# Attention of batches 1 to 3 in steps of two tiles, with q and k turned four tiles at a time

## The chip, the cores and the metric

One core of one Trainium2 chip runs the whole program. The metric is the device time of one execution in microseconds (us); three executions of the kernel before took 1161.79, 1163.22 and 1163.64 us, median 1163.22.

## The reference

The program computes an attention with a sparse mask and feeds its output to a mixture of experts. All data are float32.

```python
# B, H, S, D = 4, 8, 768, 64; n_global, n_local = 8, 96
scores = q @ k.transpose(0, 1, 3, 2) / sqrt(D)
rel = pos[:, None] - pos[None, :]
is_global = pos[None, :] < n_global
is_local = (rel >= 0) & (rel < n_local)
dist = where(is_global & ~is_local, n_local, abs(rel))
scores = where(is_global | is_local, scores - slopes[head] * dist, -1e9)
a = exp(scores - max(scores));  a = a / (sum(a) + 1e-9)
x = (a @ v) -> (B * S, H * D) = (3072, 512)

# E, F = 4, 1024
p = domain_probs / (sum(domain_probs) + 1e-9)
out = sum over e of p[:, e] * (relu(x @ w1[e]) @ w2[e])
```

Since a position looks back at most 95 places and at 8 global columns, a tile of 128 queries needs the 128 keys of its own tile, 96 of the tile before and the global ones: 256 columns.

## The kernel before

**Stages.** The attention of batch 0 runs first (`first_attention`, up to about 60 us). Then the mixture of batches 0 and 1 runs, and the attention of batches 1 to 3 (`attention`, lines 419 to 503) is emitted between its pieces, to about 644 us. The mixture of batches 2 and 3 follows without attention (`turned_batch`). The change touches the middle stage alone.

**The mixture in the middle stage.** A unit is one expert and a quarter of its hidden columns. `first(i)` does seven products of a Strassen-like scheme, each six matmuls of 384 columns into a tile `pm` of the pool `ps_mm` (four buffers, one PSUM bank each); VectorE adds and ScalarE applies the relu. `second(i)` does six groups of six matmuls of 512 columns, each summed by VectorE into `acc`. `first` yields seven times a unit and `second` six times. At these yields the outer loop (lines 1344 to 1377) draws further steps of `attention`: the steps (`count`) are spread evenly over the yields, `span - ONSTEPS` = 385 of them.

**A job of the attention** is one batch and one pair of heads; there are 12. A pair fills the 128 partitions (two heads of 64). q and k are loaded with positions on the partitions and turned by TensorE transposes (`transpose_half`, three tiles at a time, into a buffer of the pool `bank.pt`), then split into a high and a low part in `qs` and `ks` (`prepare_q`, `prepare_k`): ScalarE copies the high part, VectorE subtracts for the low part; once a job VectorE also copies the global keys behind each tile of keys. `scores` does 12 matmuls for two tiles of queries, each from half the array's rows (64 partitions), into two banks of one buffer each (`bank.psa`, `bank.psb`). `softmax` has VectorE add the bias and take the row's extreme, ScalarE take the exponential, VectorE the reciprocal and ScalarE scale. `turn` transposes the weights of one tile (four transposes, two for tile 0) into `bank.pt` (two buffers), and ScalarE copies them to `pT`. `weigh` multiplies three tiles with v, each matmul filling half the array's columns.

**The order in a job.** A step called `flow` handles one tile in each of three states: it emits the scores of a new pair of tiles, then the turn of the tile that is three steps old, then the softmax of the tiles one and two steps old. A job takes 12 steps: q half 0, k half 0, q half 1, tile 0 (with its scores), tile 1, k half 1, an empty step, tile 2 (scores), tile 3, an empty step, tile 4 (scores), tile 5. When six tiles are turned, `leave` emits the 44 products with v; this falls into the next job's step of tile 0, ahead of its scores. The next job's q and k are asked for at the step of tile 5, v at the step of tile 0. All 12 jobs make 149 steps.

**The order on the engines.** The program lists each engine's instructions in one order. In the first stage the code fixes that order itself (`Ordered.on`). From the outer loop's seventh yield on this is off, and the framework's planner orders the instructions by its own cost estimates, with the emitted order as priority.

Of the kernel before, what the change touches and what calls it, by code (L numbers as in the profile page):

```python
# [9 lines left out]
F32 = mybir.dt.float32  # L10
# [4 lines left out]
ALU = mybir.AluOpType  # L15
# [10 lines left out]
def f32(ap):  # L26
    return ap.bitcast(F32)
# [159 lines left out]
def attn_moe_kernel(ctx: ExitStack, tc, q, k, v, n_global, n_local, domain_probs, w1, w2, out):  # L187
# [108 lines left out]
    def load(A, src, b, pr, name):  # L296

        nat = A.nat.tile([P, NQT, 2, D], F32, name=name)
        for j in range(2):
            sy.dma_start(nat[:, :, j, :], src[b, 2 * pr + j].rearrange("(t p) d -> p t d", p=P))  # L300
        return nat

    def transpose_half(A, nat, hf):
        tp = A.pt.tile([P, 512], F32, name="pt")
        for t in range(TPH):
            te.transpose(tp[:, t * P : (t + 1) * P], nat[:, hf * TPH + t].rearrange("p j d -> p (j d)"), ident)
        return tp

    def prepare_q(A, nat, hf, got):

        tp = transpose_half(A, nat, hf)
        if hf == 0:
            got["q"] = A.qs.tile([P, 2, S], F32R, name="qs")
        hi, lo = (got["q"][:, n, hf * HALF : (hf + 1) * HALF] for n in range(2))
        ac.activation(hi, tp[:, :HALF], AF.Copy, scale=-SCALE)
        ve.scalar_tensor_tensor(lo, tp[:, :HALF], -SCALE, f32(hi), op0=ALU.mult, op1=ALU.subtract)

    def prepare_k(A, nat, hf, got):

        tp = transpose_half(A, nat, hf)  # L320
        tpv = tp[:, :HALF].rearrange("p (t c) -> p t c", c=P)
        if hf == 0:
            got["k"] = A.ks.tile([P, 2, NQT, PL], F32R, name="ks")
        ks = got["k"]
        hi, lo = (ks[:, n, hf * TPH : (hf + 1) * TPH, :P] for n in range(2))
        ac.copy(hi, tpv)
        ve.tensor_tensor(lo, tpv, f32(hi), op=ALU.subtract)
        if hf == 0:
            ve.tensor_copy(ks[:, :, :, P:], f32(ks[:, :, 0:1, :NGLOB]).to_broadcast([P, 2, NQT, NGLOB]))

    def scores(ts, got):


        pss = [pool.tile([P, 2, 2 * P], F32, name="ps") for pool in (bank.psa, bank.psb)]
        for i, t in enumerate(ts):
            c0 = max(t - 1, 0) * PL + (0 if t == 0 else NGLOB)
            for n, (qn, kn) in enumerate(((0, 0), (0, 1), (1, 0))):
                for j in range(2):
                    own = slice(j * D, (j + 1) * D)
                    te.matmul(  # L340
                        pss[j][:, i],
                        got["q"][own, qn, t * P : (t + 1) * P],
                        got["k"][own, kn].rearrange("p t c -> p (t c)")[:, c0 : c0 + 2 * P],
                        start=(n == 0),
                        stop=(n == 2),
                    )
        return pss

    def softmax(A, new, old):


        if old:
            pb, zsum = old["pb"], old["zsum"]
        if new:
            t, pr, ps = new["t"], new["pr"], new["ps"]
            cols = slice(0, P) if t == 0 else slice(0, 2 * P)
            bcol = slice(2 * P, 3 * P) if t == 0 else slice(0, 2 * P)
            new["pcol"] = pcol = slice(P, 2 * P) if t == 0 else slice(0, 2 * P)
            nmax = A.small.tile([P, 2], F32, name="nmax")
            new["zsum"] = A.small.tile([P, 2], F32, name="zsum")  # L360
            new["pb"] = A.pb.tile([P, 2, 2 * P], F32, name="pb")
        for j in range(2):
            if new:
                e = new["pb"][:, j, pcol]
                ve.tensor_tensor_reduce(
                    e, ps[j][:, t % 2, cols], bias["n"][:, 2 * pr + j, bcol], 1.0, 3.0e38, ALU.add, ALU.min,
                    nmax[:, j : j + 1],
                )
                ac.activation(
                    e, e, AF.Exp, bias=nmax[:, j : j + 1], scale=-1.0, accum_out=new["zsum"][:, j : j + 1]  # L370
                )
            if old:
                if j == 1:
                    ve.reciprocal(zsum, zsum)
                else:
                    ac.activation(zsum, zsum, AF.Copy, bias=1e-9)
        if old:
            for j in range(2):
                p = pb[:, j, old["pcol"]]
                ac.activation(p, p, AF.Copy, scale=zsum[:, j : j + 1])  # L380

    def turn(bank, A, tile_, copy):

        t, pb = tile_["t"], tile_["pb"]
        pt = bank.pt.tile([P, 2, 2, P], F32, name="pt")
        pT = A.pT.tile([P, 2, 2, P], F32, name="pT")
        w0 = 1 if t == 0 else 0
        for w in range(w0, 2):
            for j in range(2):
                te.transpose(pt[:, w, j, :], pb[:, j, w * P : (w + 1) * P], ident)  # L390
        copy(pT[:, w0:], pt[:, w0:])
        tile_["pT"] = pT
# [16 lines left out]
    def weigh(bank, three, own):  # L409

        px = bank.pt.tile([P, 512], F32, name="pt")
        for i, tile_ in enumerate(three):
            products_with_v(px, i, tile_)
        t = tile_["t"]
        ac.copy(own[:, (t - TPH + 1) * P : (t + 1) * P], px[:, :HALF])
# [3 lines left out]
    def attention(A):  # L419


        jobs = [(b, pr) for b in range(1, B) for pr in PAIRS]
        tiles, turned, scored = [None] * 4, [], {}
        nats, gots = {}, {}

        def leave(b, pr):
            if b == 1:
                if b not in xs:
                    xs[b] = xp.tile([P, NPAIR, S], F32, name="x")
                own = xs[b][:, pr]  # L430
            else:
                own = A.xt.tile([P, S], F32, name="xt")
            weigh(bank, turned[:TPH], own)
            weigh(bank, turned[TPH:], own)
            turned.clear()
            if b > 1:
                to = xd[(b, pr)] = dp.tile([P, S], F32, name=f"x{b}_{pr}")
                sy.dma_start(to, own)

        def flow(new=None):  # L440

            one, two, three, four = tiles
            if four:
                turned.append(four)
            if len(turned) == NQT:
                leave(*four["job"])
            if new:
                t = new["t"]
                if t % 2 == 0:
                    scored["ps"] = scores((t, t + 1), gots[new["job"]])  # L450
                new["ps"] = scored["ps"]
            if three:
                turn(bank, A, three, ac.copy)
            softmax(A, one, two)
            tiles[:] = [new, one, two, three]

        def start(b, pr):

            nats[(b, pr)] = {n: load(A, src, b, pr, n) for n, src in (("q", q), ("k", k))}

        def start_v(b, pr):

            vt, vg = (A.natv.tile([P, 2, NQT, D], F32, name=n) for n in ("v", "vg"))
            load_v(vt, vg, b, pr)
            nats[(b, pr)]["v"], nats[(b, pr)]["vg"] = vt, vg

        def prepare(nat, got):

            got["v"] = nat
            prepare_q(A, nat["q"], 0, got)  # L470
            yield 1
            prepare_k(A, nat["k"], 0, got)
            yield 1
            prepare_q(A, nat["q"], 1, got)
            yield 1
            prepare_k(A, nat["k"], 1, got)
            yield 1
            yield 1
            yield 1

        start(*jobs[0])
        yield
        for m, job in enumerate(jobs):
            cur = gots[job] = {}
            prep = prepare(nats[job], cur)
            for _ in range(3):
                next(prep)
                flow()
                yield
            for t in range(NQT):  # L490
                for _ in range({2: 2, 4: 1}.get(t, 0)):
                    next(prep)
                    flow()
                    yield
                if t == NQT - 1 and m + 1 < len(jobs):
                    start(*jobs[m + 1])
                flow({"t": t, "pr": job[1], "job": job, **cur})
                if t == 0:
                    start_v(*job)
                yield  # L500
        while any(tiles):
            flow()
            yield

    def load_x(b):
        xs[b] = xp.tile([P, NPAIR, S], F32, name="x")
# [834 lines left out]
        po.tensor_copy(flag, fits)  # L1341

    per = E * NPR
    count = (B - 1) * NPAIR * (6 + NQT) + 5
    span = (TURNED * 13 * per - 12) * 0.97
    Ordered.on = True
    att = attention(A)
# [73 lines left out]
```

## Time and profile before

| | |
|---|---|
| median of three runs | 1163.22 us |
| profiled execution, own time | 1164.4 us |
| its span | 1162.6 us |
| mean granted TensorE clock | 0.999 |
| busy share: TensorE, its weight loads, VectorE, ScalarE, GpSimd | 98%, 91%, 74%, 45%, 41% |
| TensorE busy by stretch: 0 to 60, 60 to 88, 88 to 630, 630 to 645, 645 to 1162.6 us | 52.84, 25.09, 541.89, 15.00, 509.20 us |

A row of the profile names an engine (PE is TensorE's matmuls, PEld its weight loads, DVE is VectorE, ACT is ScalarE, POOL is GpSimd, SP issues DMAs), an operation, the tile written and those read, and a count. All rows say line 42, the helper through which every instruction is emitted, so a row is known by its tiles: `ps<-ks,qs` are scores, `pt<-ident,q`, `pt<-ident,k` and `pt<-ident,pb` are transposes of q, of k and of weights, `pt<-pT,v` and `pt<-pT,vg` are products with v, `pm<-xT,w1s` and `pm<-xB,w1s` products of `first`, `pm<-w2s,h` those of `second`. Matmuls are pipelined, and the length of a row of matmuls reaches past the start of the next row; where a row took its time is read from the starts.

### The profile page before, as it was taken

The page shows a single profiled execution, that of the slowest core. Times are in us where ns is not written, and L with a number is a line of the kernel's source. Part 1 is how long each engine was busy: PE and PEld are TensorE (multiplying, and loading weights), DVE is VectorE, ACT ScalarE, POOL GpSimd, SP SyncE. Part 2 cuts the span into 40 slices and gives each one's busy share as a digit, 9 for nine tenths or more (in the row PEclk, how much of TensorE's full clock was granted, in tenths as well). Part 3 has the DMA queues.
Part 4 walks back from the last instruction along what each step waited for, and adds up shares of the span by engine and source line. Part 5 has one row for each costly group of instructions (what it writes and reads, how often), then busy time and mean ns, then how long its engine had stood idle before and what let it go on. Part 6 is the DMA issues. An engine that isn't in the chain of part 4 may idle for free.

```text
span 1162.6 us, 19037 instructions
## 1 busy us (share of the span) xinstructions
PE 1144.0 (98%) x7101; PEld 1055.4 (91%) x7101; DVE 866.1 (74%) x1653; ACT 528.1 (45%) x1303; POOL 478.1 (41%) x435
## 2 busy tenths in 40 slices
PE   8999999999999999999999999999999999999998
PEld 6778898989888988888888899999999899999996
DVE  6977676676677766766676787898889678988984
ACT  6747565665655545545454314222224253222231
POOL 5757544554411000000000257676672377766710
PEclk9999999999999999999999999999999999999999
DMA  8569677867677675665656665666766656666632
GB/s 193 146 210 354 233 272 222 267 222 234 243 230 206 217 227 163 206 197 175 201 169 225 225 242 189 224 220 229 277 219 248 220 202 231 217 231 218 217 118 94
DMA packets 170116, 250.98 MB, mean 216 GB/s; under 512 B 108480, under 2 KB 144416, under 8 KB 157216
## 3 DMA queue, kind: packets, MB, share of 16 engines
q1 hardware_dynamic: 164976, 233.43, 60.3%
q0 software_dynamic: 4032, 14.68, 3.3%
q10 hardware_dynamic: 1008, 1.57, 0.4%
q8 instruction: 58, 0.95, 0.3%
q14 instruction: 42, 0.34, 0.1%
HBM read 194.04 MB, written 55.62 MB: 215 GB/s over the span
## 4 chain that ended last, share of the span: by engine, by line
PE 90%; DVE 6%; DMA 1%; ACT 1%; issue 1%; SPq 1%; POOL 0%; DVEq 0%; ACTq 0%
PE pm L42 63%; PE pq L42 16%; PE pt L42 7%; PE ps L42 4%; DVE form L42 1%; DVE sumT L42 1%; DVE hB L42 1%; SPq L42 1%; DVE pT L42 0%; DMA raw<-in_moe_w_dram 0%; DVE x L42 0%; DMA raw_n<-in_n_local_dram 0%; DMA first_k<-in_k_dram 0%; DVE pb L42 0%; DVE sumB L42 0%
## 5 line engine op out<-in xcount | busy, mean ns | idle before, releaser
L42 PE MATMUL pm<-xT,w1s 128*128 128x384 f32 x1536 | 302.9, 337 | 0.8 <-DVE h L42 0.5
L42 PE MATMUL pm<-w2s,h 128*128 128x512 f32 x1152 | 279.9, 395 | 1.6 <-DVE h L42 1.6
L42 PEld LDWEIGHTS pm<-xT,w1s 128*128 128x128 f32 x1536 | 267.6, 188 | 2.7 <-DVE h L42 1.6
L42 PEld LDWEIGHTS pm<-w2s,h 128*128 128x128 f32 x1152 | 212.0, 188 | 44.6 <-POOL sums L42 1.6
L42 PE MATMUL pm<-xB,w1s 128*128 128x384 f32 x1152 | 226.9, 338 | 2.6 <-DVE hB L42 2.0
L42 PEld LDWEIGHTS pm<-xB,w1s 128*128 128x128 f32 x1152 | 200.7, 188 | 7.0 <-DVE hB L42 3.5
L42 DVE SCALAR_TENSOR_TENSOR acc<-pm,prob,acc 128x512 f32<-128x512 f32 x180 | 134.1, 749 | 68.7 <-PE pm L42 68.2
L42 POOL TENSOR_TENSOR xT<-x,xT 128x768 fp32r<-128x768 f32 x4 | 7.4, 1843 | 316.1 <-ACT xT L42 316.1
L42 PE MATMUL pq<-form,w2s 128*128 128x384 f32 x672 | 125.8, 334 | 0.0
L42 POOL TENSOR_TENSOR raw<-raw 128x512 f32<-128x512 f32 x56 | 79.3, 1416 | 99.6 <-DMA raw<-in_moe_w_dram 96.3
L42 PEld LDWEIGHTS pq<-form,w2s 128*128 128x128 f32 x672 | 117.3, 188 | 0.0
L42 ACT ACTIVATE pb<-pb,nmax 128x256 f32<-128x256 f32 (+1 forms) x192 | 92.5, 483 | 35.0 <-DVE nmax L42 34.4
L42 PE MATMUL pq<-form,w2f 128*128 128x384 f32 x504 | 94.1, 334 | 0.0
L42 PEld LDWEIGHTS pq<-form,w2f 128*128 128x128 f32 x504 | 88.0, 188 | 0.0
L42 ACT ACTIVATE h<-pm 128x384 fp32r<-128x384 f32 x128 | 61.9, 488 | 50.2 <-DVE pm L42 47.4
L42 ACT CAST form<-hB 128x768 fp32r<-128x768 f32 x70 | 57.0, 837 | 60.5 <-DVE hB L42 60.4
L42 POOL TENSOR_TENSOR w2s<-raw,w2s 128x512 fp32r<-128x512 f32 x46 | 63.0, 1382 | 49.6 <-ACT w2s L42 48.4
L42 ACT COPY p<-pm 128x384 f32<-128x384 f32 x64 | 30.5, 477 | 113.9 <-PE pm L42 113.9
L42 DVE SCALAR_TENSOR_TENSOR h<-pm,h 128x384 fp32r<-128x384 f32 x128 | 70.4, 551 | 9.7 <-ACT h L42 7.5
L42 DVE CUSTOM_DVE_ANT_0 pb<-ps,nbias 128x256 f32<-128x256 f32 (+1 forms) x144 | 50.2, 397 | 33.9 <-PE ps L42 27.2
L42 POOL TENSOR_TENSOR form<-hB,form 128x768 fp32r<-128x768 f32 x28 | 57.3, 2045 | 25.5 <-ACT form L42 25.5
L42 DVE TENSOR_TENSOR form<-hB,form 128x768 fp32r<-128x768 f32 x42 | 59.3, 1440 | 11.1 <-ACT form L42 10.9
(149 smaller groups left out, 1697.8 us busy)
## 6 DMA issues: line engine op xcount, KB each, us to landing
w1s<-kept SPq DMA_DIRECT2D x48, 1792.0 KB, 8.2
kept<-w1s SPq DMA_DIRECT2D x16, 1792.0 KB, 8.4
w2s<-kept SPq DMA_DIRECT2D x84, 256.0 KB, 5.0
w2s<-kept SPq DMA_DIRECT2D x20, 1024.0 KB, 4.9
raw<-in_moe_w_dram SPq DMA_DIRECT2D x32, 512.0 KB, 4.2
kept<-w2s SPq DMA_DIRECT2D x16, 1024.0 KB, 6.3
raw<-in_moe_w_dram POOLq DMA_DIRECT2D x28, 512.0 KB, 7.4
v<-in_v_dram SPq DMA_DIRECT2D x12, 384.0 KB, 5.4
```

What stands on the lines that cost most here:

```text
L42: ins = fn(*args, **kwargs)
```

## The change

The attention of batches 1 to 3 gets a new order; its matmuls, softmax and products with v are the same in number and shape.

- `transpose_half`, `prepare_q` and `prepare_k` give way to `turn_qk(bank, nat, got, part)`. Part 0 turns tiles 0 to 3 of q into the bank of `psa` and of k into the bank of `psb`, those that the scores use too; part 1 turns tiles 4 and 5 of both into one buffer of `ps_mm`. Behind them come two copies on ScalarE and two subtractions on VectorE, and with part 0 the copy of the global keys.
- `flow` gives way to a loop over pairs of tiles, four steps each. First step: products with v of the job before (first pair only), the pair's scores, the turn of all older tiles not yet turned, part 1 of q and k (first pair only), the softmax's first half for the first tile. Second step: the second tile's first half and the first tile's second half. Third step: the second tile's second half, and, for the first pair, the loads of the next job. Fourth step: nothing, but for the last pair the turn of its two tiles and part 0 of the next job's q and k.
- A job still takes 12 steps; all 12 take 147.

```diff
-    def transpose_half(A, nat, hf): ...
-    def prepare_q(A, nat, hf, got): ...
-    def prepare_k(A, nat, hf, got): ...
+    def turn_qk(bank, nat, got, part):
+        if part == 0:
             got["q"] = A.qs.tile([P, 2, S], F32R, name="qs")
             got["k"] = A.ks.tile([P, 2, NQT, PL], F32R, name="ks")
+            ts = range(4)
+            tps = [pool.tile([P, 4 * P], F32, name="ps") for pool in (bank.psa, bank.psb)]
+        else:
+            ts = range(4, NQT)
+            tp = ps_mm.tile([P, 4 * P], F32, name="pm")
+            tps = [tp[:, : 2 * P], tp[:, 2 * P :]]
+        t0, t1 = ts[0], ts[-1] + 1
+        for tp, m in zip(tps, ("q", "k")):
+            for t in ts:
+                te.transpose(tp[:, (t - t0) * P : (t - t0 + 1) * P], nat[m][:, t]..., ident)
+        tpq, tpk = tps[0], tps[1].rearrange("p (t c) -> p t c", c=P)
+        qh, ql = (got["q"][:, n, t0 * P : t1 * P] for n in range(2))
+        kh, kl = (got["k"][:, n, t0:t1, :P] for n in range(2))
+        ac.activation(qh, tpq, AF.Copy, scale=-SCALE)
+        ac.copy(kh, tpk)
+        ve.scalar_tensor_tensor(ql, tpq, -SCALE, f32(qh), op0=ALU.mult, op1=ALU.subtract)
+        ve.tensor_tensor(kl, tpk, f32(kh), op=ALU.subtract)
+        if part == 0:
+            ks = got["k"]
             ve.tensor_copy(ks[:, :, :, P:], f32(ks[:, :, 0:1, :NGLOB]).to_broadcast([P, 2, NQT, NGLOB]))
...
-        def flow(new=None): ...
-        def prepare(nat, got): ...
         start(*jobs[0])
         yield
+        turn_qk(bank, nats[jobs[0]], gots[jobs[0]], 0)
+        yield
         for m, job in enumerate(jobs):
+            then = jobs[m + 1] if m + 1 < len(jobs) else None
+            own = tiles[job] = []
+            for t in range(0, NQT, 2):
+                if t == 0 and m > 0:
+                    leave(jobs[m - 1])
+                pss = scores((t, t + 1), gots[job])
+                for tile_ in own:
+                    if "pT" not in tile_:
+                        turn(bank, A, tile_, ac.copy)
+                two = [{"t": t + n, "pr": job[1], "v": nats[job], "ps": pss} for n in range(2)]
+                own += two
+                if t == 0:
+                    turn_qk(bank, nats[job], gots[job], 1)
+                softmax(A, two[0], None)
                 if t == 0:
                     start_v(*job)
                 yield
+                softmax(A, two[1], two[0])
+                yield
+                softmax(A, None, two[1])
+                if t == 0 and then:
+                    start(*then)
+                yield
+                if t == NQT - 2:
+                    for tile_ in two:
+                        turn(bank, A, tile_, ac.copy)
+                    if then:
+                        turn_qk(bank, nats[then], gots[then], 0)
+                yield
+        leave(jobs[-1])
+        yield
...
-    count = (B - 1) * NPAIR * (6 + NQT) + 5
+    count = (B - 1) * NPAIR * 2 * NQT + 3
```

## Rows read from the trace of the kernel before

**Rows 1.** The page, part 1: busy us, share of the span, instructions.

```profile
PE 1144.0 (98%) x7101; PEld 1055.4 (91%) x7101; DVE 866.1 (74%) x1653; ACT 528.1 (45%) x1303; POOL 478.1 (41%) x435
```

**Rows 2.** Windows: busy us of PE, PEld, DVE, ACT, POOL; clock; DMA, GB/s.

```profile
88.00:630.00 542.00, 541.89 (x3474) 482.28 (x3475) 374.12 (x898) 309.74 (x863) 134.11 (x132) 1.00 0.68 225
48.00:57.00 9.00, 6.63 (x81) 5.14 (x81) 8.93 (x30) 6.10 (x21) 7.01 (x8) 1.00 0.01 3
```

**Rows 3.** Waits of TensorE, 88 to 630 us: us in total, times, longest.

```profile
PE ps L42 <- DVE ks L42: 0.4, 1, 0.4
```

**Rows 4.** Timeline of TensorE: start us, length us, engine, what, count.

```profile
99.73 0.97 PE L42 MATMUL ps<-ks,qs 64*128 64x256 f32 x12
...
114.40 0.60 PE L42 MATMUL pt<-ident,pb 128*128 128x128 f32 x4
114.76 1.29 PE L42 MATMUL pm<-xT,w1s 128*128 128x384 f32 x6
115.89 1.55 PE L42 MATMUL pm<-w2s,h 128*128 128x512 f32 x6
...
296.36 0.97 PE L42 MATMUL ps<-ks,qs 64*128 64x256 f32 x12
297.27 0.66 PE L42 MATMUL pt<-ident,pb 128*128 128x128 f32 x4
297.68 4.37 PE L42 MATMUL pm<-w2s,h 128*128 128x512 f32 x18
301.88 0.60 PE L42 MATMUL pt<-ident,pb 128*128 128x128 f32 x4
...
306.84 1.20 PE L42 MATMUL pm<-xB,w1s 128*128 128x384 f32 x6
307.88 0.49 PE L42 MATMUL pt<-ident,k 128*128 128x128 f32 x3
308.21 0.60 PE L42 MATMUL pt<-ident,pb 128*128 128x128 f32 x4
...
315.75 0.44 PE L42 MATMUL pt<-pT,v 128*64 128x128 f32 x4
...
318.30 0.98 PE L42 MATMUL ps<-ks,qs 64*128 64x256 f32 x12
319.21 4.37 PE L42 MATMUL pm<-w2s,h 128*128 128x512 f32 x18
323.42 1.23 PE L42 MATMUL pm<-xB,w1s 128*128 128x384 f32 x6
...
622.82 0.98 PE L42 MATMUL ps<-ks,qs 64*128 64x256 f32 x12
...
638.64 0.60 PE L42 MATMUL pt<-ident,pb 128*128 128x128 f32 x4
```

**Rows 5.** VectorE by form, 88 to 630 us: busy us, mean ns, idle.

```profile
L42 DVE SCALAR_TENSOR_TENSOR acc<-pm,prob,acc 128x512 f32<-128x512 f32 x158 | 118.1, 749 | 62.3 <-PE pm L42 61.8
...
L42 DVE CUSTOM_DVE_ANT_0 pb<-ps,nbias 128x256 f32<-128x256 f32 x120 | 45.1, 419 | 8.5 <-PE pt L42 6.1 <-PE ps L42 1.9
...
L42 DVE CAST ks<-ks 128x384 fp32r<-128x384 f32 x11 | 5.5, 501 | 0.2
```

**Rows 6.** ScalarE by form, 88 to 630 us.

```profile
L42 ACT COPY pT<-pt 128x512 f32<-128x512 f32 x58 | 33.9, 585 | 25.9 <-PE pt L42 25.9
```

**Rows 7.** Timeline of all engines around the first scores.

```profile
87.05 0.92 DVE L42 CAST ks<-ks 128x384 fp32r<-128x384 f32 x1
...
88.11 0.98 PE L42 MATMUL ps<-ks,qs 64*128 64x256 f32 x12 [0.43 <-DVE ks L42]
```

**Rows 8.** Timeline of all engines at the tightest use of the product buffers.

```profile
344.59 2.35 PE L42 MATMUL pm<-xT,w1s 128*128 128x384 f32 x12
...
350.18 0.56 DVE L42 SCALAR_TENSOR_TENSOR h<-pm,h 128x384 fp32r<-128x384 f32 x1
...
350.79 1.43 PE L42 MATMUL pm<-w2s,h 128*128 128x512 f32 x5
```

More of the change, by code (lines that the diff above doesn't have):

```diff
@@ L301, in load @@
         return nat
[L303 to L312, printed above, removed]
-            got["q"] = A.qs.tile([P, 2, S], F32R, name="qs")
-        hi, lo = (got["q"][:, n, hf * HALF : (hf + 1) * HALF] for n in range(2))
-        ac.activation(hi, tp[:, :HALF], AF.Copy, scale=-SCALE)
-        ve.scalar_tensor_tensor(lo, tp[:, :HALF], -SCALE, f32(hi), op0=ALU.mult, op1=ALU.subtract)
@@ L318, in prepare_k @@
[L318 to L322, printed above, removed]
-            got["k"] = A.ks.tile([P, 2, NQT, PL], F32R, name="ks")
[L324 to L328, printed above, removed]
+    def turn_qk(bank, nat, got, part):
+        if part == 0:
+            got["q"] = A.qs.tile([P, 2, S], F32R, name="qs")
+            got["k"] = A.ks.tile([P, 2, NQT, PL], F32R, name="ks")
+            ts = range(4)
[7 more added lines that the diff above has]
+            for t in ts:
+                te.transpose(
+                    tp[:, (t - t0) * P : (t - t0 + 1) * P], nat[m][:, t].rearrange("p j d -> p (j d)"), ident
+                )
+        tpq, tpk = tps[0], tps[1].rearrange("p (t c) -> p t c", c=P)
[7 more added lines that the diff above has]
+            ks = got["k"]
@@ L422, in attention, with leave @@
         jobs = [(b, pr) for b in range(1, B) for pr in PAIRS]
-        tiles, turned, scored = [None] * 4, [], {}
-        nats, gots = {}, {}
-        def leave(b, pr):
+        nats, gots, tiles = {}, {}, {}
+        def leave(job):
+            b, pr = job
             if b == 1:
@@ L432, in leave @@
                 own = A.xt.tile([P, S], F32, name="xt")
-            weigh(bank, turned[:TPH], own)
-            weigh(bank, turned[TPH:], own)
-            turned.clear()
+            weigh(bank, tiles[job][:TPH], own)
+            weigh(bank, tiles[job][TPH:], own)
             if b > 1:
@@ L438, in leave @@
                 sy.dma_start(to, own)
[L440 to L455, printed above, removed]
         def start(b, pr):
             nats[(b, pr)] = {n: load(A, src, b, pr, n) for n, src in (("q", q), ("k", k))}
+            gots[(b, pr)] = {}
         def start_v(b, pr):
@@ L465, in start_v @@
             nats[(b, pr)]["v"], nats[(b, pr)]["vg"] = vt, vg
[L467 to L479, printed above, removed]
         start(*jobs[0])
         yield
+        turn_qk(bank, nats[jobs[0]], gots[jobs[0]], 0)
+        yield
         for m, job in enumerate(jobs):
[L484 to L497, printed above, removed]
+            then = jobs[m + 1] if m + 1 < len(jobs) else None
[12 more added lines that the diff above has]
+                softmax(A, two[0], None)
                 if t == 0:
@@ L500, in attention @@
                 yield
-        while any(tiles):
-            flow()
-            yield
+                softmax(A, two[1], two[0])
[12 more added lines that the diff above has]
+        yield
     def load_x(b):
```

## The prediction

> **What bounds the kernel now.** I read the page first: TensorE (PE) is busy 98% of the span, VectorE (DVE) 74%, ScalarE (ACT) 45% [rows 1]. That is an average over unlike stages, so next came a table of stretches. The attention of batches 1 to 3, the code that changes, runs from about 88 to 644 us beside the first two batches of the mixture. From 88 to 630 us PE is busy 541.89 of 542.00 us at a granted clock of 1.00, DVE 374 and ACT 310 us [rows 2]. The reader is to see that this stage has no idle PE time to win. The waits of PE there say the same: one wait, 0.4 us, the first scores for the keys [rows 3]. So a saving must come from fewer nanoseconds of PE for the same matmuls, and any new wait of PE costs its full length.
>
> The third view is the timeline of PE by itself [rows 4], where the difference of two starts is the PE time that a run really takes (the lengths shown overlap and are no measure). Prices from it:
> - A transpose inside a run: the three of k start at 307.88, the next run at 308.21: 0.33 / 3 = 0.110 us.
> - Four transposes alone between products: 114.76 - 114.40 = 0.36 us, and the six products behind them take 115.89 - 114.76 = 1.13 us where six with nothing foreign ahead take 307.88 - 306.84 = 1.04. So 0.36 + 0.09 = 0.45, against 4 x 0.110 = 0.44. Over the 14 such runs (114.40 the first, 638.64 the last) the same difference is 0.458 on average, and 0.474 if twelve products behind are counted. A run that stands alone costs 0.02 us over its transposes (0.01 to 0.035).
> - Four transposes directly behind scores: scores, transposes and 18 products take 301.88 - 296.36 = 5.52 us; scores and 18 products without transposes 323.42 - 318.30 = 5.12. So 0.40 us for four, 0.04 less than 4 x 0.110: coming back from the half-array scores to full-array work is paid once either way (over the 24 such runs, 99.73 to 622.82, the average is 0.393). A run behind scores saves 0.04 us (0.035 to 0.045).
>
> **The change, part by part.** For each of the 12 jobs (three batches, four pairs of heads) the matmuls stay the same: three runs of 12 scores, 44 products with v, and 34 transposes (22 of weights, 12 of q and k). What moves is the grouping of the transposes.
>
> *Runs.* Before, a job has eight runs: q, k with a tile, q with a tile, k, the two of tile 0, and the turn of tile 5 stand alone or with each other (six), and two stand behind scores (both kinds are in [rows 4]). After: behind the first scores 4 (q and k of tiles 4 and 5), behind the second 6, behind the third 8, and one run of 16 by itself (tiles 4 and 5, and the next job's q and k of tiles 0 to 3). So six alone and two behind scores become one alone and three behind scores: 5 x 0.02 + 1 x 0.04 = 0.14 us a job, 12 x 0.14 = 1.7 us. From the low ends 5 x 0.01 + 0.035 = 0.085, 1.0 us; from the high ends 5 x 0.035 + 0.045 = 0.22, 2.6 us. Scores stay three runs, entered and left as before, and products with v still stand directly ahead of the first scores. I take 2.2 us, halfway between 1.7 and 2.6, since the higher price counts more of the products behind.
>
> *Copies of q and k.* Two of 512 columns and two of 256 on each of DVE and ACT in place of four of 384. DVE: 512 columns cost 749 ns in a mixture row, 256 about 419 [rows 5], so 2 x 0.75 + 2 x 0.42 = 2.34 us a job; four of 384 at 0.56 (a row of that shape is in [rows 8]) were 2.24. ACT: 585 ns for 512 [rows 6]. The 0.1 us a job are hidden: DVE idles 168 of 542 us.
>
> *The first part of q and k gathered in one place.* Their copies and the copy of the global keys (0.50 us on average [rows 5], 0.92 at its first use [rows 7]) now all stand between the run of 16 and the next scores. Chain: ACT turns to q behind up to two weight copies (one of them already under way), 2 x 0.6 for q and k, then DVE 0.75 for the k subtraction and 0.5 for the globals, some 0.5 of hand-over: about 3.2 us. Until the scores PE has one step and the products with v: 147 steps over the 385 sub-steps that pace them is 2.6 products a step, at 1.04 to 1.4 us (4.21 / 3) [rows 4], 2.7 to 3.6 us, plus 318.30 - 315.75 = 2.55. So 5.3 to 6.2 us against 3.2: cost 0, with 2 us to spare for whatever else DVE has queued. If the cover is gone, PE waits for the difference 11 times. At the first job there are no products with v; there the scores already waited 0.43 us [rows 7], and 0 to 1 us is possible; I keep 0.4.
>
> *Softmax directly behind its scores.* DVE's reduction is now emitted in the step of the scores, not one step later, so it can stand in DVE's queue ahead of the mixture's sums while PE is still at the scores. PE spends that time on the scores themselves (0.9 us) and on 0.4 to 0.9 us of transposes, needing no sum: cost 0, at most what the next part says.
>
> *One of the four product buffers.* q and k of tiles 4 and 5 go through a buffer of the pool that the mixture's products rotate in. For the three products behind it the rotation is three deep in place of four. The tightest place now: the product behind 344.59 has its buffer released by DVE at 350.18 + 0.56 = 350.74, and the product four later starts at 350.79 [rows 8]. With one place less this would have been over 1 us late. But the loan always begins behind 3.5 us of products with v and scores (319.21 - 315.75), in which DVE catches up; 0 is the value, and 0 to 1.0 us a job the range (a product of 1.04 us less the 0.05 left).
>
> *Loads.* q and k of the next job are asked for five steps earlier; nothing waits for them now [rows 3]. The v loads stay. The DMAs stand in the SP queue behind the v loads of the same job instead of the last tile's work, and the buffers that they fill are free by then. 0.
>
> *Clock.* The run of 16 holds PE for 16 x 0.11 = 1.8 us with nothing but transposes, and the first step of a job holds it 2.55 + 0.9 + 0.4 = 3.9 us without a full-array product. From 48 to 57 us PE did only transposes, half-array products and scores, 6.6 of 9 us busy, and the granted clock was 1.00 [rows 2]. The Trainium skill says in "TensorE: Matmul & The Clock Gate", Part 4, that transposes do not count as activity that keeps the clock up, which would speak against long runs of them. By that rule the clock would fall around these stretches; this trace does not agree, since its first stage ran mostly on such work at full clock.
>
> **Sum.** -2.2 us by the runs, 0 for the rest, with a possible 0.4 either way at the first job: the profiled execution (span 1162.6, own time 1164.4) would go to 1160.4 and 1162.2. The median of the runs is 1163.22, 1.2 below the profiled one; the same step from there gives 1161.0 us. 0.2% of it is 2.3 us, about what a measurement tells from no change.
>
> **The rivals.**
> 1. *The runs do not stand where the code puts them.* In this stage the code leaves the order on each engine to the planner's own costs, and a transpose whose tile it thinks late goes behind a product instead. For it: only a trace can show the order that comes out. Against: all 24 runs that the code before emits behind scores stand there. If all four runs of a job stood alone, they would cost 4 x 0.02 = 0.08 over their transposes, against 6 x 0.02 - 2 x 0.04 = 0.04 now: 12 x 0.04 = 0.5 us more, 1163.7 us, no change that can be told.
> 2. *Slower: scores wait for the gathered q and k.* Place: first scores of each job. It decides from the point where DVE has over 2 us of other work queued ahead of the copy of the global keys. For it: in a mixture unit's first half DVE has 11 operations of 0.56 us [rows 8] (seven sums and four low parts) in 7 x 1.04 = 7.3 us of PE, 85% of the time without any attention. Against: the run of 16 and the products with v give DVE 4.3 us without new sums. Say 1 us more than that at each of 11 jobs: 11 - 2.2 = 8.8, 1172 us.
> 3. *Slower, milder: the lent buffer.* PE waits up to 1.0 us in the half of the jobs whose loan falls into the first half of a unit: 6 x 1.0, less 2.2, gives +3.8, 1167 us. For it the 0.05 us left at the tightest place [rows 8], against it the catch-up above.
> 4. *The clock falls* to 1.2 GHz around the stretches without full-array products: at half the rate the 1.8 + 3.9 us of each job double, 12 x 5.7 = 68 us more, less 2.2: 1229 us. The granted 1.00 of 48 to 57 us [rows 2] is against it. The rule of the Trainium skill named under *Clock* is what would bring it about.
>
> **How the numbers follow.** Forecast 0.62, rival 1 0.14, rival 2 0.09, rival 3 0.14, rival 4 0.01. The forecast's own range is 1160.2 to 1162.6 (2.6 and 1.0 us, 0.4 at the first job). The start and the end of the kernel, where nearly all of PE's 18 idle us lie, can move by some tenths more. The range that holds 8 in 10 goes from 1159.2 into rival 3: 1165.5; rivals 2 and 4 and a part of 3 stay outside. Faster by over 0.2% means below 1160.9, next to the forecast itself: a little over half of its chance, 0.36. Within 0.2%: the rest of it, 0.26, rival 1, and the smaller waits of rival 3, 0.04: 0.44. Slower: rivals 2 and 4 and the rest of rival 3: 0.20.
>
> **What would show it.** In the timeline of PE, four runs of transposes a job instead of eight, three of them starting right where scores end, and 0.40 us or less for each four of them. In the stage's window, PE still busy all the time and shorter by some 2 us. Rival 1 shows as runs between products; rival 2 as waits of the scores for ks or qs; rival 3 as waits of products for a DVE or ACT reader, at the first step of a job; rival 4 as a clock below 1.00. The prediction is wrong if the time moves by more than 3 us down, which no price here allows, or if PE waits more than 2 us in the stage.

## The result, and the profile after

The changed kernel takes 1173.67 us (median of 5 runs, 1173.14 to 1175.69), the kernel before 1163.22 us beside it (5 runs, 1161.79 to 1164.62). The ratio is 1.0092, its 95% interval 1.0081 to 1.0103: slower by 10.5 us. The forecast, 1161.0 us, and its range, up to 1165.5, were wrong. The profiled execution of the changed kernel has an own time of 1173.88 us, a span of 1172.1 and a mean granted clock of 0.995; before it was 1164.4, 1162.6 and 0.999.

The page of the changed kernel, part 1 (busy us, share, instructions) and the clock row of part 2, stands against [rows 1]:

```profile
PE 1146.9 (98%) x7101; PEld 1059.0 (90%) x7101; DVE 869.5 (74%) x1653; ACT 521.0 (44%) x1303; POOL 480.4 (41%) x435
...
PEclk9989999999999999999999999999999999999999
```

The shares look as before. What gives the loss away is one 8 in the clock's third slice, where the page of before has a 9. The table of stretches of the changed kernel goes closer (the stretches are those of [rows 2], then two short ones; the columns are the stretch, its length, each engine's busy us, the granted clock, the DMA share and GB/s):

```profile
core 0: us, PE busy (x) PEld busy (x) DVE busy (x) ACT busy (x) POOL busy (x), PEclk, DMA share, GB/s
60.00:88.00 28.00, 20.95 (x123) 18.25 (x121) 18.05 (x39) 12.31 (x27) 13.89 (x20) 0.88 0.72 217
88.00:630.00 542.00, 539.02 (x3439) 480.73 (x3438) 370.09 (x882) 297.83 (x847) 135.95 (x133) 1.00 0.67 223
...
82.00:86.00 4.00, 4.00 (x18) 3.90 (x19) 0.85 (x2) 1.37 (x4) 2.93 (x5) 0.56 0.78 245
...
362.00:365.00 3.00, 2.70 (x6) 2.04 (x7) 2.03 (x4) 1.13 (x2) 1.47 (x1) 0.50 0.02 5
```

From 60 to 88 us TensorE is busy 20.95 us, where before it was 25.09. In the stage, where before it stood idle for 0.1 us [rows 2], 3 us are idle. And there are two stretches at about half of the clock: 0.56 and 0.50, the lower of the two levels (1.2 GHz) nearly throughout.

The waits of TensorE in the stage, against [rows 3] (us in total, times, longest):

```profile
PE pm L42 <- DVE h L42: 2.4, 1, 2.4
PE pt L42 <- ACT pb L42: 0.5, 1, 0.5
```

No wait for ks or qs, none that comes back once a job: one wait of 2.4 us and one of 0.5. So the loss is not spread over the twelve jobs. To place it I compared, for the same matmul of the mixture in both traces (the n-th), when it starts. This table is worked out from the starts in the two timelines, in us:

```
start before   start after   later by   between the two places
     71.47         71.89       +0.43
    102.52        108.50       +5.98    first job's q and k: +5.55
    342.13        347.34       +5.21    some five jobs: -0.77
    387.25        397.30      +10.04    end of the mixture's first batch: +4.83
    643.81        653.46       +9.64    the other jobs: -0.40
```

Two single places cost 5.6 and 4.8 us. The rest of the stage gains 1.2 us by these starts, the way that was forecast and about half of its size.

**The first place, the first q and k.** The timeline of TensorE in the changed kernel (start us, length us, engine, operation, count, and in brackets the idle time before it with what ended it):

```profile
75.08 1.33 PE L42 MATMUL pm<-xB,w1s 128*128 128x384 f32 x6 [0.82 <-DVE h L42]
81.86 1.09 PE L42 MATMUL ps<-ident,q 128*128 128x128 f32 x4 [5.45 <-DMA q<-in_q_dram]
82.74 0.64 PE L42 MATMUL pm<-ident,q 128*128 128x128 f32 x2
83.03 1.31 PE L42 MATMUL pm<-xT,w1s 128*128 128x384 f32 x3
...
86.00 1.31 PE L42 MATMUL pm<-w2s,h 128*128 128x512 f32 x5
```

and the same place in the kernel before:

```profile
75.49 1.21 PE L42 MATMUL pm<-xT,w1s 128*128 128x384 f32 x6
78.00 4.83 PE L42 MATMUL pm<-w2s,h 128*128 128x512 f32 x20 [1.30 <-DVE h L42]
82.66 0.49 PE L42 MATMUL pt<-ident,q 128*128 128x128 f32 x3
```

Before, q is turned behind a unit's last product and 20 matmuls with `w2s`, which cover its load. After, the turn of q stands ahead of that product (`pm<-xT,w1s` at 83.03) and of all the `w2s` matmuls: TensorE stands idle for 5.45 us until q has landed, and the product, which before started without a wait, comes behind the turn. The load itself is hardly later than before. SyncE asks for it at 70.58 us (70.16 before), in the changed kernel's rows:

```profile
69.98 0.51 SPq L42 DMA_DIRECT2D kept<-w1s  x1
70.58 1.23 SPq L42 DMA_DIRECT2D q<-in_q_dram  x2
```

Ahead of it in the queue is a store of 1.8 MB. With the wait comes the slow stretch: the four transposes take 82.74 - 81.86 = 0.88 us, twice the 0.44 of [rows 4]. From 81.86 to 86.00 TensorE does twelve transposes and six products of 384 columns, 4.14 us against 12 x 0.110 + 1.04 = 2.36 by the prices of [rows 4]. So 5.45 - 1.30 for the longer wait and 4.14 - 2.36 for the clock: 5.9 us, near the 5.6 of the table.

**The second place, the seam of the mixture's batches.** At about 342 to 387 us the function `blocks` forms the operands of batch 1's mixture (`xT` and `xB`) out of `x`, the output of the attention; I call this the seam. The hidden values `h` are kept as a high and a low part, like q and k, and the `w2s` matmuls need both. TensorE in the changed kernel:

```profile
359.52 0.39 PE L42 MATMUL pt<-ident,pb 128*128 128x128 f32 x2
362.30 2.93 PE L42 MATMUL pm<-w2s,h 128*128 128x512 f32 x6 [2.40 <-DVE h L42]
365.03 0.80 PE L42 MATMUL pt<-ident,pb 128*128 128x128 f32 x4
```

VectorE and GpSimd in the changed kernel, from two timelines of one engine each:

```profile
359.23 2.56 DVE L42 TENSOR_TENSOR x<-x 128x768 f32<-128x768 f32 x1 [1.57 <-POOL xB L42]
361.70 1.01 DVE L42 SCALAR_TENSOR_TENSOR h<-pm,h 128x384 fp32r<-128x384 f32 x2
...
357.34 1.85 POOL L42 TENSOR_TENSOR xB<-x,xB 128x768 fp32r<-128x768 f32 x1 [7.59 <-ACT xB L42]
359.15 1.82 POOL L42 TENSOR_TENSOR xT<-x,xT 128x768 fp32r<-128x768 f32 x1
360.93 2.55 POOL L42 TENSOR_TENSOR xB<-x,xB 128x768 fp32r<-128x768 f32 x1
```

and VectorE in the kernel before:

```profile
352.63 0.56 DVE L42 SCALAR_TENSOR_TENSOR h<-pm,h 128x384 fp32r<-128x384 f32 x1 [0.16 <-ACT h L42]
...
353.64 0.54 DVE L42 SCALAR_TENSOR_TENSOR h<-pm,h 128x384 fp32r<-128x384 f32 x1
354.10 2.06 DVE L42 SCALAR_TENSOR_TENSOR acc<-pm,prob,acc 128x512 f32<-128x512 f32 x3
356.07 0.94 DVE L42 TENSOR_TENSOR x<-x 128x768 f32<-128x768 f32 x1
```

Before, the subtraction in place on `x` stands behind the low parts of `h` and three sums. After, it stands ahead of the last two low parts. It writes what GpSimd is still reading for `xB`, so it waits 1.57 us, then takes 2.56 instead of 0.94 us, and the next six `w2s` matmuls wait 2.40 us for those low parts. The six then go by at 365.03 - 362.30 = 2.73 us, where six take 1.36 at full clock (227 ns each); the clock of the stretch is the 0.50 above. 0.52 + 2.40 + 1.37 is 4.3 of the 4.8 us of this place.

**What the runs of transposes gave.** TensorE in the changed kernel, at the second and third scores of the first job:

```profile
113.73 0.98 PE L42 MATMUL ps<-ks,qs 64*128 64x256 f32 x12
114.64 1.09 PE L42 MATMUL pt<-ident,pb 128*128 128x128 f32 x8
115.49 0.77 PE L42 MATMUL pm<-xT,w1s 128*128 128x384 f32 x3
...
124.58 1.04 PE L42 MATMUL pt<-ident,pb 128*128 128x128 f32 x8
125.46 0.60 PE L42 MATMUL ps<-ident,q 128*128 128x128 f32 x4
125.90 0.60 PE L42 MATMUL ps<-ident,k 128*128 128x128 f32 x4
126.25 0.94 PE L42 MATMUL pm<-w2s,h 128*128 128x512 f32 x3
```

Eight transposes start where the scores end, and 16 stand together. A section is a stretch of matmuls that are not the mixture's, between two of its products. I priced every section from the starts, less the mixture's products with their usual 173 and 227 ns (six products behind each section counted). Medians in us, 10 to 23 of each: before, a job is 0.359 (q), 0.786 (k and a tile), 0.785 (q and a tile), 3.684 (products with v and scores), 0.358 (k), 0.247 (two of tile 0), 2 x 1.525 (scores and four) and 0.456 (four alone), 9.73 in all. After, it is 4.072 (products with v, scores, four), 1.736 (scores and six), 1.948 (scores and eight) and 1.773 (sixteen), 9.53. That is 0.20 us a job, and 2.2 for the eleven whole jobs.

### The profile page after: what moved, and what is told of

Same layout as the page of the kernel before. It is cut to its first block, busy times and chain, and to the rows that moved or that the text cites. A ratio compares the mean times of both kernels' runs of the same rounds, so it can differ in the third digit from the quotient of the medians.

```text
span 1172.1 us, 19086 instructions
## 1 busy us (share of the span) xinstructions
PE 1146.9 (98%) x7101; PEld 1059.0 (90%) x7101; DVE 869.5 (74%) x1653; ACT 521.0 (44%) x1303; POOL 480.4 (41%) x435
## 3 DMA queue, kind: packets, MB, share of 16 engines
q10 hardware_dynamic: 1008, 1.57, 0.4%
## 5 line engine op out<-in xcount | busy, mean ns | idle before, releaser
L42 PE MATMUL pm<-w2s,h 128*128 128x512 f32 x1152 | 274.8, 394 | 2.7 <-DVE h L42 2.7
L42 PEld LDWEIGHTS pm<-w2s,h 128*128 128x128 f32 x1152 | 214.7, 189 | 46.4 <-DVE h L42 3.3
L42 PE MATMUL pm<-xB,w1s 128*128 128x384 f32 x1152 | 224.5, 337 | 1.2 <-DVE h L42 0.8
L42 ACT COPY pT<-pt 128x512 f32<-128x512 f32 (+2 forms) x73 | 37.8, 549 | 77.4 <-PE pt L42 76.8
L42 DVE TENSOR_TENSOR form<-hB,form 128x768 fp32r<-128x768 f32 x42 | 62.5, 1516 | 11.1 <-ACT form L42 10.9
```

Source lines behind the costliest of these rows:

```text
L42: ins = fn(*args, **kwargs)
```

## The experiments

The theory after the result: the runs bring the 2 us; the two waits with their slow stretches cost the 10 to 11, and both come from the order that the planner chose, not from the new code of the jobs. Rivals: the loss comes from the new shape of a job itself (the lent buffer, the softmax or the copies crowding VectorE), or one of the two places is only a follower of the other. The kernel before has a median of 1162.55 us beside the first four experiments and of 1162.97 beside the last two, against 1163.22 beside the changed kernel; a difference between two kernels that were not timed side by side is uncertain by about that much.

**Two empty steps before the first turn.** The load of q and k gets two steps more of room; the jobs stay as changed. The edit does more than that. The first scores come back to the fifth step, where they stood before the change (the change has them in the third), and with 149 steps in place of 147 every later step of the attention moves against the mixture: by about five sub-steps at the first job, three at the seam and none at the end.

```diff
         start(*jobs[0])
         yield
+        yield
+        yield
         turn_qk(bank, nats[jobs[0]], gots[jobs[0]], 0)
-    count = (B - 1) * NPAIR * 2 * NQT + 3
+    count = (B - 1) * NPAIR * 2 * NQT + 5
```

> Two empty steps between the request for the first job's q and k and their turn; all else as in the changed kernel. Theory A (the loss is two single waits of TensorE: 5.5 us for the first q at 76 us, and some 3.3 us at the seam to the mixture of batch 1 at 355 to 362 us, each with a stretch at 1.2 GHz behind it; the new order itself gains 1.5 to 2.2 us): in this program the first q stands behind 20 matmuls of the mixture again, and at the seam the subtraction on x stands behind the low parts of h, so both waits go: 1173.7 - 5.6 - 5.2 = 1161 to 1163 us, 0 to 2 us below the kernel before, clock 0.999. Rival B (gathered q and k, the lent buffer and the bursts make TensorE wait in all jobs): the two empty steps leave 11 of 12 jobs as they are, 1172 to 1174 us.

Measured: 1161.90 us (11 runs) against 1162.55 (21 runs): 0.9993 (0.9984 to 1.0002). Both places are mended at once. The table of stretches of this kernel for the stage, and its TensorE and VectorE timelines at the two places:

```profile
88.00:630.00 542.00, 542.00 (x3478) 484.61 (x3475) 373.22 (x899) 303.48 (x863) 134.47 (x132) 1.00 0.68 226
```

```profile
77.39 4.83 PE L42 MATMUL pm<-w2s,h 128*128 128x512 f32 x20 [1.38 <-DVE h L42]
82.06 0.60 PE L42 MATMUL ps<-ident,q 128*128 128x128 f32 x4
```

```profile
351.91 0.53 DVE L42 SCALAR_TENSOR_TENSOR h<-pm,h 128x384 fp32r<-128x384 f32 x1
...
353.68 0.94 DVE L42 TENSOR_TENSOR x<-x 128x768 f32<-128x768 f32 x1
```

TensorE is busy all 542 us. q is turned behind the 20 matmuls, as before the change, and the subtraction on `x` stands behind the last low part of `h`. By the same comparison of starts this kernel is 0.47 us ahead of before at 71 us and 2.24 ahead at 644: the stage gains 1.8 us, with every job as in the change. So the jobs themselves lose nothing, and 11.8 of the changed kernel's 1173.67 us (11.5 by the two ratios) hang on where the steps fall and on the order that the planner makes of them. Which of the moved steps mends the seam, this run does not say. The next three leave every step but the first request where the changed kernel has it.

**The first load earlier.** The changed kernel with the first q and k asked for ahead of the 1.8 MB store.

```diff
-                if done == ONSTEPS:
+                if done == 3:
                     next(att)
+                if done == ONSTEPS:
                     check_sizes()
```

> The first job's q and k are asked for four sub-steps earlier, which puts them ahead of a 1.8 MB store in the SP queue; the seam at 355 us keeps its order. Theory A: the wait for the first q falls from 5.5 to under 1.5 us and with it the half-rate stretch to 85 us: 4.5 to 5.6 us less, 1168 to 1169 us; the wait at 355 to 362 us stays. If the place of the turn, not the landing of q, is what costs (rival: the turn holds back the products that stand behind it whatever its data do), at most 1 us less: 1173 us.

Measured: 1167.74 us (4 runs), 1.0043 (1.0028 to 1.0058), 5.9 us less than the changed kernel. TensorE in this kernel:

```profile
77.11 0.63 PE L42 MATMUL ps<-ident,q 128*128 128x128 f32 x4
...
79.42 1.33 PE L42 MATMUL pm<-xT,w1s 128*128 128x384 f32 x6 [1.46 <-DVE h L42]
```

The turn still stands ahead of the product, but q is there: no wait for it, and 0.63 us for four where the slow stretch showed 1.09. The product behind it waits 1.46 us for VectorE to read out a product buffer: part 1 of q has taken one of the four just ahead of it (`pm<-ident,q` at 77.58). That looks like the mechanism of rival 3, once, at the first job; the 1.30 us that the first `w2s` matmul waited before the change are gone in return, and by starts the first place costs nothing here (2.06 us behind the kernel before at 71 us, left over from a slow stretch at 10 to 17 us of this execution, and 2.00 at 103). The wait of 2.4 us at the seam is unchanged. So the first place is worth about the 5.6 us that the comparison of starts gave it, and the second does not hang on it. The place of the turn alone costs nothing; it costs where q has not landed.

**The seam alone.** The changed kernel with the one low part that GpSimd makes for batch 1 made by VectorE, so that the subtraction has nobody to wait for.

```diff
-        rest(po, "B22", b22)
+        rest(ve if b == 1 else po, "B22", b22)
```

> At the seam to the mixture of batch 1 the low part of B22 is made by VectorE, not GpSimd, so VectorE's subtraction on x has no GpSimd to wait for; the start is as in the changed kernel. Theory A: TensorE's wait of 2.4 us for h at 362 us goes, or most of it, and with it the six matmuls at 427 ns: 3 to 5 us less than the changed kernel, 1168.5 to 1170.5 us, the wait of 5.5 us at the first q stays. Rival: the wait for h comes from ScalarE's late relu, not from VectorE's queue: then h is as late, 1173 us.

Measured: 1169.89 us (4 runs), 1.0060 (1.0045 to 1.0075), 3.8 us less than the changed kernel. VectorE in this kernel:

```profile
358.97 0.56 DVE L42 SCALAR_TENSOR_TENSOR h<-pm,h 128x384 fp32r<-128x384 f32 x1
360.08 0.56 DVE L42 SCALAR_TENSOR_TENSOR h<-pm,h 128x384 fp32r<-128x384 f32 x1 [0.55 <-ACT h L42]
...
362.55 0.95 DVE L42 TENSOR_TENSOR x<-x 128x768 f32<-128x768 f32 x1
```

The low parts come first, the subtraction takes 0.95 us, and TensorE does not wait for `h` there. The planner has put the subtraction behind the low parts again, so this run takes away the order and the wait for GpSimd together; what each costs by itself is not separated. By starts the seam costs 0.7 us in place of 4.8; what is left is near the 0.5-us wait for `pb`, which stays. In the profiled execution the first place costs 6.7 us in place of 5.6 (TensorE waits 6.0 us for q), so 4.1 us come back at the seam and 1.1 are lost at the start; the medians show 3.8.

**Both together.**

> e2 and e3 together, every step of the attention at the place it has in the changed kernel. Theory A: the two gains add, 8 to 10.5 us less than the changed kernel: 1163 to 1165.5 us. Rival B: a loss of over 5 us against the kernel before stays.

Measured: 1163.22 us (10 runs), 1.0006 (0.9997 to 1.0016): 10.5 us less than the changed kernel, where the two alone gave 5.9 and 3.8. They add up to within 1 us, so neither is a follower of the other, and with every job at its place the new jobs lose nothing. The waits of TensorE from 60 to 630 us and two rows of its timeline show what is left over the kernel with the two empty steps:

```profile
PE pm L42 <- DVE h L42: 2.1, 4, 1.5
PE pt L42 <- ACT pb L42: 0.5, 1, 0.5
```

```profile
77.36 1.31 PE L42 MATMUL pm<-xT,w1s 128*128 128x384 f32 x6 [1.45 <-DVE h L42]
...
80.23 3.40 PE L42 MATMUL pm<-w2s,h 128*128 128x512 f32 x9
```

Nine `w2s` matmuls in 3.33 us (the next row starts at 83.56) in place of 2.04: a short slow stretch, behind a wait of 1.45 us like the 1.46 us that no slow stretch followed in the kernel with the load earlier. The other thing left is the small wait at the seam. The waits for `h` are no larger than with the two empty steps (2.2 us in the same stretch).

**Runs taken apart.** The kernel with the two empty steps, with no run behind scores: all turns of weights moved to a pair's fourth step, and part 1 of q and k one step behind the first scores.

```diff
-                for tile_ in own:
-                    if "pT" not in tile_:
-                        turn(bank, A, tile_, ac.copy)
...
-                if t == 0:
-                    turn_qk(bank, nats[job], gots[job], 1)
                 softmax(A, two[0], None)
...
                 yield
+                if t == 0:
+                    turn_qk(bank, nats[job], gots[job], 1)
...
-                if t == NQT - 2:
-                    for tile_ in two:
-                        turn(bank, A, tile_, ac.copy)
-                    if then:
-                        turn_qk(bank, nats[then], gots[then], 0)
+                for tile_ in two:
+                    turn(bank, A, tile_, ac.copy)
+                if t == NQT - 2 and then:
+                    turn_qk(bank, nats[then], gots[then], 0)
```

> As e1, but the transposes leave the scores: the weights of every pair are turned in the pair's fourth step, and tiles 4 and 5 of q and k one step behind the first scores. Theory A (a run of transposes costs 0.02 us over its transposes alone and saves 0.04 behind scores): three runs a job lose the scores, 12 x 3 x 0.06 = 2.2 us more than e1, and so about 1 us more than the kernel before; in the trace the stage from 60 to 644 us loses e1's gain of 1.8 us. Rival (the gain came from fewer, longer runs alone, or from elsewhere): within 0.7 us of e1 in the stage.

Measured: 1165.38 us (10 runs) against 1162.97 (19 runs), 1.0023 (1.0013 to 1.0033). It lies 2.4 us above the kernel before, the one that it is made from 0.65 below: 3.1 us more (3.5 by the two ratios), where 2.2 was expected. TensorE in this kernel:

```profile
100.13 0.97 PE L42 MATMUL ps<-ks,qs 64*128 64x256 f32 x12
101.03 5.73 PE L42 MATMUL pm<-w2s,h 128*128 128x512 f32 x24
...
109.75 1.03 PE L42 MATMUL pt<-ident,pb 128*128 128x128 f32 x8
110.54 1.31 PE L42 MATMUL pm<-xT,w1s 128*128 128x384 f32 x6
```

Here no run stands behind scores. The sections cost 1.140 (scores), 0.678 (six) and 0.892 (eight) apart, and 1.736 and 1.948 joined (in the changed kernel): 0.08 us less for each joined run. The products with v, scores and four cost 3.678 + 0.471 apart and 4.072 joined, again 0.08. Three joined runs a job are 0.24 us, 2.9 us for twelve jobs. Part of the measured 3.1 is another thing: TensorE stands idle 1.2 us in this kernel's stage (busy 540.78 of 542), 0.7 of it a wait for `h` at the seam. Joining is real; its size is 2 to 3 us in all.

**The lent buffer given back.** The kernel with the two empty steps, with part 1 of q and k in a buffer of `bank.pt` in place of one of the four product buffers.

```diff
-            tp = ps_mm.tile([P, 4 * P], F32, name="pm")
+            tp = bank.pt.tile([P, 4 * P], F32, name="pt")
```

> As e1, but tiles 4 and 5 of q and k go through a buffer of the transposes' pool, not through one of the mixture's four product buffers. Theory A: the loan costs nothing, so within 0.7 us of e1, stage time the same, no wait of products in either. Rival (the lent buffer costs up to 1 us in half the jobs): 2 to 6 us less than e1.

Measured: 1161.40 us (10 runs) against 1162.97, 0.9986 (0.9976 to 0.9996). TensorE in this kernel:

```profile
131.33 0.98 PE L42 MATMUL ps<-ks,qs 64*128 64x256 f32 x12
132.23 0.44 PE L42 MATMUL pt<-ident,q 128*128 128x128 f32 x2
132.51 0.38 PE L42 MATMUL pt<-ident,k 128*128 128x128 f32 x2
```

The run stands in the same place with another buffer. At 669 us this kernel is 1.91 us ahead of before, the one with the loan 2.27: with this order the loan costs nothing. This is the one version whose interval lies below 1, by 1.6 us in the median. It was not timed side by side with the kernel with the loan, so which of the two is better stays open.

## Why the prediction was wrong

- **Runs, -2.2 us: right in kind, and in size near enough.** By sections 0.20 us a job and 2.2 in all; by starts -1.8 in the kernel where nothing else happens and -1.2 outside the two places of the changed kernel. In the whole time it is not clear of the noise there (0.9984 to 1.0002). Four runs a job, three of them where scores end, so rival 1 is out. The split was off: joining a run with scores saves 0.08 us, where I had 0.04 over the transposes and 0.02 for a run alone, 0.06 together.
- **Copies, softmax, gathered q and k: 0, right.** TensorE waits for no ks or qs in the stage. Rival 2 gave 1172 us, near the time that came, but its mechanism did not happen: the number fits by chance, and only the waits tell the two apart.
- **The lent buffer: 0, right in the stage**; rival 3 is out there by the last experiment. Its wait shows once, ahead of the stage, in the two kernels with the load earlier (1.46 and 1.45 us).
- **"At the first job ... 0 to 1 us is possible; I keep 0.4": the step that failed.** It was 5.6 us. I asked whether the scores would wait for ks, and took for granted that the turn of q would stay behind the 20 `w2s` matmuls that cover its load. The code emits that turn one step behind the request in both kernels; the cover was the planner's choice. The change also puts the first scores two steps nearer to the request. The rows of [rows 4] begin at 99.73 us; the stretch with the first load was read only for the scores [rows 7].
- **"0 for the rest": failed as well, at the seam, 4.8 us.** I priced the jobs and not the other work that shares the engines' order. The prediction named the planner in rival 1, but only for where the transposes stand, with 0.5 us.
- **Loads: 0, and "nothing waits for them now" [rows 3]: failed at the first job.** Those rows begin at 88 us, behind the first load, and the term weighed only the next jobs' loads (by the code these come eight steps earlier, not five). The first is asked for 0.4 us later than before, and the turn of q now stands where it must wait for it.
- **Clock: 0 for the runs, right, and yet it cost.** The 16 transposes in a row run at the granted 1.00 of the stage, so rival 4 is out. By the rule that the prediction names under *Clock* it could have fallen there, and it did not; a run is only 1.77 us long, though, and the stretch from 48 to 57 us had 44 half-array products beside its transposes, and no scores, so neither settles that rule. It fell at the two waits. The Trainium skill says in "TensorE: Matmul & The Clock Gate", section "Part 1: The HAM clock gate", that an idle TensorE goes back to the slower clock and activity releases it; the trace agrees, with 0.56 behind 5.45 us of waiting and 0.50 behind 2.40. Those stretches cost about 1.8 and 1.4 us on top of the waits. The length of a wait does not tell alone: 1.45 us had a slow stretch behind it in one kernel, 1.46 us at the same place none in another.
- "The prediction is wrong ... if PE waits more than 2 us in the stage": it waits 2.4 once there, and 5.45 ahead of it.

Shown by the runs: that the two waits with their slow stretches make the loss, that each can be taken away by itself with every job left at its place, and that both go when the steps are paced as before the change and the first scores stand at the fifth step again. Not shown: why the planner puts the turn of q and the subtraction where it does. Its costs were not varied, and the two empty steps move the whole attention against the mixture, so they do not say whether a single edit at the start would reach the seam.

## What to carry to other kernels

Where a planner orders the engines, regrouping one stream of work also re-orders the other work beside it. With TensorE full, price the edit, and then line up the same instruction in both traces over the whole span and find the jumps, before any theory of the edit itself. A wait of a full TensorE costs its length and can cost a slow stretch behind it (1.8 and 1.4 us here). Give the first load of a stage room in the code, and do not leave it to the luck of the order: asking for it ahead of a large store gave back 5.9 us here.

## What was not expected of the hardware

VectorE's subtraction of two 128x768 operands takes 0.94 to 0.96 us by itself and took 2.56 us at 359.23, begun 0.08 us behind a GpSimd operation that ran from 359.15 to 360.97; what is left behind that end is 361.79 - 360.97 = 0.82 us. It looks as if it did nothing until GpSimd was through. GpSimd's next operation, at 360.93, took 2.55 us against 1.85 for the same shape at 357.34, as if it had waited for VectorE in turn. The Trainium skill says in "SBUF — State Buffer", section "SBUF: two separate sides", that GpSimd and a VectorE operation with two inputs in SBUF share a pair of ports that the one that starts first keeps for its whole instruction; the trace agrees, with those numbers.
